# Means of v by TensorE, summary rows in one product a head, a later index step and another tile for the hidden row, in an attention and two-MoE kernel

## The chip, the core and the metric

The kernel runs on one core of a Trainium2 chip. A core has engines that run side by side, each through its own list of instructions in a fixed order: TensorE (PE, with its weight loads as PEld), VectorE (DVE), ScalarE (ACT), GpSimd (POOL) and SyncE (SP), whose queue here issues most of the loads. They meet by semaphores. The metric is the device time of one execution in microseconds, as the median of several runs.

## The reference

Three layers over 2 x 768 tokens with 512 columns (8 heads of 64). First an attention of two parts: each query sees the keys within 15 places of it, and one summary for each of 24 blocks of 32 tokens. A block's key summary is the maximum, its value summary the mean:

```python
k_sum = k.reshape(B, H, nb, block, D).max(axis=3)
v_sum = v.reshape(B, H, nb, block, D).mean(axis=3)
scores_s = scale * np.einsum('bhsd,bhnd->bhsn', q, k_sum) + np.log(block)
scores_all = np.concatenate([scores_l_m, scores_s], axis=-1)   # softmax over both
return np.matmul(a, np.concatenate([v, v_sum], axis=2))
```

Then a dense layer, `max(x @ w1, x @ w2, x @ w3) @ w_out`, and a mixture of 8 experts: a token with a positive skip score goes through `relu(xc @ w1[e]) @ w2[e]` of its best expert, times the gate's weight, plus itself; other tokens stay as they are.

## The kernel before

**Work units.** The 1536 tokens are four groups u of 384 (groups 0 and 1 are the first sequence, b = 0). In attention the heads go in four pairs p, two heads on 128 partitions. Per group and pair: keys and queries are loaded, `scores` makes products of 64 queries with 96 keys and 24 summaries, softmax follows (`ttr` on VectorE, `ex` on ScalarE, `rec` on VectorE, `norm` on POOL), `turn` transposes the weights on TensorE, `turned` copies them to SBUF (ps), and `pv` multiplies them with the values. For `pv` a block's values are a window tile vx of 120 rows: 96 rows of v, loaded (L227), and below them 24 rows of summaries, which ScalarE copies in once for each of six blocks (`fill_v`, L250). Those summaries come from the whole v of the pair, transposed (`load_v`, 384 KB), summed by VectorE (`sum_v`, L205), turned by TensorE (`sum_t`, L210) and scaled by ScalarE (`sum_o`). They serve both groups of a sequence.

**The dense layer** runs over the result in high and low float32r parts: 18 chains of 12 products a group (`chain`, L367), each after its weights are split on ScalarE, POOL and VectorE (`w_c1` to `w_c5`, L334 to L360) from 512 KB chunks. In the first group's first chain each part (`cp`) follows one head pair. To keep TensorE busy while there is little for it, 63 products of a zero tile are made at the start (`warm_up`, L185), in 20 groups.

**What sets the order.** Up to the experts, each piece of work is an entry (`op`) with an engine, a duration, a key, what it comes after, and the buffers it takes and frees. `arrange` simulates the engines with those durations, always takes the ready piece with the smallest key, and the order that comes out is the order in which every engine gets its instructions. On the DMA queue a piece without a free buffer holds up all behind it. The warm-up groups are such pieces too, with keys 0 to 19; `att` gives the pieces of attention.

**Experts.** Written out by hand: the most frequent expert's tokens go in pairs of 128-token tiles (`pair`) and a last `single`, another expert's in a `single`, and up to 32 tokens left over from a third expert (the remainder) in `tail`, spread over the steps of a pair: `tail_x` (L995 to L997) makes an index on VectorE and fetches rows by POOL. With FAST2 the pair has a second remainder. In `single` the hidden row, 128 x 512 for each half, is written by ScalarE to `hr`, turned by TensorE and split.

Of the kernel before, what the change touches and what calls it, by code (L numbers as in the profile page):

```python
# [8 lines left out]
F32 = mybir.dt.float32  # L9
# [9 lines left out]
B, H, S, D = 2, 8, 768, 64  # L19
P = 128  # L20
NPR = H // 2
QB = 64
NBK = S // QB
KW = 96
NS = 24
KT = KW + NS
G = 384
BPG = G // QB
TPG = G // P
# [116 lines left out]
def build(tc, a, out):  # L146
    nc = tc.nc
# [3 lines left out]
    psM = ctx.enter_context(tc.tile_pool(name="psM", bufs=3, space=PSUM))  # L151
# [4 lines left out]
    ax_ = actx.enter_context(tc.tile_pool(name="ksvs", bufs=1, side="right"))  # L156
# [44 lines left out]
    def sum_v(b, p):  # L201
# [3 lines left out]
        nc.vector.tensor_reduce(vs[:, KW:], vt, AX.X, ALU.add)  # L205
        ST["vs", b, p] = vs

    def sum_t(b, p):
        ST["pvs", b, p] = psM.tile([P, 512], F32, name="pm")
        nc.tensor.transpose(ST["pvs", b, p][:KT, :P], ST["vs", b, p], ident)  # L210
# [89 lines left out]
    def pv(u, p):  # L300
        vx = ST["vx", u, p]
        po = psO.tile([P, G], F32, name="po")
        for i in range(BPG):
            for h in range(2):
                nc.tensor.matmul(po[64 * h:64 * h + 64, i * QB:(i + 1) * QB], vx[:, i, 64 * h:64 * h + 64],
                                 ST["ps", u, p, h][:, i * QB:(i + 1) * QB], start=True, stop=True)
        ST["po", u, p] = po
# [258 lines left out]
    ONE = {}  # L566
# [205 lines left out]
    def op(name, eng, dur, key, fn, *args, after=(), take=(), uses=(), lag=0.0):  # L772
        OPS.append(dict(name=name, eng=eng, dur=dur, key=key, fn=fn, args=args, after=after, take=take, uses=uses, lag=lag))

    def att(u, p, s, t, o):
        b, half = divmod(u, 2)
        e = (u, p)
        pre = s - 12 if u else -100.0 + 10 * p
        if half == 0:
            ek = EARLY_KV.get((b, p))  # L780
            op(("lk", b, p), "DMA", 1.35, pre, load_k, b, p, take=[(ek[0] if ek else "raw", ("kt", b, p))])
            op(("sk", b, p), "DVE", 0.87, s - 3, sum_k, b, p, after=[("lk", b, p)], take=[(f"ks{p}", ("ks", b, p))],
               uses=[("kt", b, p)])
        if u == 0:
            op(("lkx",) + e, "DVE", 1.0, s - 2.5, windows, p, after=[("lk", b, p)],
               take=[(EARLY_X[e][0] if e in EARLY_X else "kx", ("kx",) + e)], uses=[("kt", 0, p)])
        else:
            op(("lkx",) + e, "DMA", 1.25, pre + 0.1, load_x, u, p, "k", take=[(EARLY_X[e][0] if e in EARLY_X else "kx", ("kx",) + e)])
        op(("lq",) + e, "DMA", 0.68, pre + 0.2, load_x, u, p, "q", take=[("qt", ("qt",) + e)])
        if half == 0:  # L790
            op(("lv", b, p), "DMA", 1.35, pre + 0.3, load_v, b, p, take=[(ek[1] if ek else "raw", ("vt", b, p))])
            op(("sv", b, p), "DVE", 0.92, s - 2, sum_v, b, p, after=[("lv", b, p)],
               take=[("vs", ("vs", b, p))], uses=[("vt", b, p)])
            op(("st", b, p), "PE", 0.2, s + 1, sum_t, b, p, after=[("sv", b, p)], take=[("pm", ("pvs", b, p))],
               uses=[("vs", b, p)])
            op(("so", b, p), "ACT", 0.17, s + 1, sum_o, b, p, after=[("st", b, p)], take=[(f"v1{p}", ("v1", b, p))],
               uses=[("pvs", b, p)])
        op(("lvx",) + e, "DMA", 1.0, pre + 0.4, load_x, u, p, "v", take=[(EARLY_X[e][1] if e in EARLY_X else "vx", ("vx",) + e)])
        op(("fk",) + e, "DVE", 0.15, s - 1, fill_k, u, p, after=[("lkx",) + e, ("sk", b, p)], uses=[("ks", b, p)])
        op(("fv",) + e, "ACT", 0.8, t, fill_v, u, p, after=[("lvx",) + e, ("so", b, p)],  # L800
           uses=[("v1", b, p)])
        for h in range(2):
            g = e + (h,)
            if h == 0:
                op(("sc",) + e, "PE", 0.8, s, scores, u, p, after=[("fk",) + e, ("lq",) + e],
                   take=[(f"{z}{i}", (z,) + e + (i,)) for z in ("sc", "pr") for i in range(2)], uses=[("kx",) + e, ("qt",) + e])
            op(("tt",) + g, "DVE", 0.61, s + 0.5 + 0.1 * h, ttr, u, p, h, after=[("sc",) + e, ("mask",)], uses=[("sc",) + g])
            op(("ex",) + g, "ACT", 1.14, s + 0.6 + 0.1 * h, ex, u, p, h, after=[("tt",) + g])
            op(("rc",) + g, "DVE", 0.36, s + 0.7 + 0.1 * h, rec, u, p, h, after=[("ex",) + g])
            op(("nm",) + g, "Pool", 0.82, s + 0.8 + 0.1 * h, norm, u, p, h, after=[("rc",) + g])  # L810
            op(("tu",) + g, "PE", 0.33, t + 0.1 * h, turn, u, p, h, after=[("nm",) + g], take=[(f"pt{h}", ("pt",) + g)],
               uses=[("pr",) + g])
            op(("td",) + g, "ACT", 0.43, t + 0.2 + 0.1 * h, turned, u, p, h, after=[("tu",) + g],
               take=[(f"ps{h}", ("ps",) + g)], uses=[("pt",) + g])
        op(("pv",) + e, "PE", 0.86, o, pv, u, p, after=[("td",) + e + (0,), ("td",) + e + (1,), ("fv",) + e],
           take=[("po", ("po",) + e)], uses=[("ps",) + e + (0,), ("ps",) + e + (1,), ("vx",) + e])
        tk = [("xh", ("xh", u)), ("xl", ("xl", u))] if p == 0 else []
        op(("ph",) + e, "ACT", 0.38, o + 0.3, put_h, u, p, after=[("pv",) + e], take=tk)
        op(("pl",) + e, "DVE", 0.51, o + 0.4, put_l, u, p, after=[("ph",) + e], uses=[("po",) + e])

    op(("mask",), "DMA", 0.5, -99.75, load_mask)
    op(("consts",), "DMA", 0.45, 30, load_consts)
    op(("tri",), "DVE", 0.15, 36, put_tri, after=[("consts",)])
    op(("table",), "Pool", 0.5, 50.0, clear_table, take=[("cx", ("table",))], lag=2.0)
# [146 lines left out]

    xn, inx, xth, xtl, ph, ptx = (M2[z] for z in ("xn", "inx", "xth", "xtl", "ph", "ptx"))
    xr, yo, xm = ([mp.tile([P, DM], F32, name=f"{z}{i}") for i in range(2)] for z in ("xr", "yo", "xm"))
    hr = [xr[1], xm[1]]
    ic, isc, im = (mp.tile([P, 2, 2], I32, name=z) for z in ("ic", "isc", "im"))
    hth, htl = ([mp.tile([P, 512], F32R, name=f"{z}{i}") for i in range(2)] for z in ("hth", "htl"))
    py = [psM.tile([P, 512], F32, name="pm") for _ in range(2)]
# [84 lines left out]

    def pair(p, t, spl=0, gen=None):
        begin(2)
        if spl:
            tail_x(spl)
        tails = TAILS2 if spl == FAST2 else TAILS
        hv = [(hth[b // 2][:, b % 2 * 2 * P:(b % 2 + 1) * 2 * P], htl[b // 2][:, b % 2 * 2 * P:(b % 2 + 1) * 2 * P])
              for b in range(4)]

        def first(f):
            ps = ph[f % 3][:, :2 * P]
            n, o = 0, f % 4 * P
            for i, r in ((0, xth), (1, xth), (0, xtl)):
                for d in range(KC1):
                    w = M2["w", p, 2 * d + f // 4][i]
                    nc.tensor.matmul(ps, w[:, o:o + P], r[:, d, :], start=(n == 0), stop=(n == 3 * KC1 - 1))  # L1077
                    n += 1
            hh, hl = hv[f % 4]
            nc.scalar.activation(hh, ps, AF.Relu)  # L1080
            nc.vector.scalar_tensor_tensor(hl, ps, 0.0, hh.bitcast(F32), ALU.max, ALU.subtract)  # L1081

        def second(f):
            hh, hl = hv[f % 4]
            wh, wl = M2["w", p, 8 + f]
            for i in range(2):
                o = i * P
                for n, (l, r) in enumerate(((hh, wh), (hh, wl), (hl, wh))):
                    nc.tensor.matmul(py[i], l[:, o:o + P], r, start=(f == 0 and n == 0), stop=(f == 7 and n == 2))  # L1089
        first(0)  # L1090
        if gen:
            nc.gpsimd.tensor_copy(inx, M2["in2"])
            fetch()
        first(1)
        for f in range(8):
            if f == 5:
                turn_x()
            if f + 2 < 8:
                first(f + 2)
            if f == 5:  # L1100
                next_x(t + 2)
            second(f)
            if gen and f < 4:
                for _ in range(2):
                    next(gen, None)
                if f == 3:
                    ids("in2", row(1))
            if spl:
                for c in PSPL[f] if spl != FAST2 else ():
                    split(c, 1 - p)  # L1110
                if f in tails:
                    tail(tails[f])
        end(2)

    def single(p, t, spl=0, last=False):
        begin(1)
        if spl:
            tail_x(spl)
# [112 lines left out]
    def most():  # L1231
# [13 lines left out]
            with tc.If(VK[0] > 8):  # L1245
                pair(0, b0 + 4)
        with tc.If((VK[0] & 1) == 0):
            single(0, l0)
        with tc.If(VK[1] > 1):  # L1249
            single(1, b1 + 1, last=True)  # L1250

    def any_ranks():
        for k in range(NE):
# [13 lines left out]
def host_inputs(inputs):  # L1267
# [2 lines left out]
    t = lambda z: np.ascontiguousarray(z.transpose(0, 1, 3, 2)).reshape(B, NPR, P, S)  # L1270
    r["qt"] = t(q)
    r["vt"] = t(v)
    r["kt"] = t(k)
    kt = np.zeros((B, NPR, P, S + 32), np.float32)
    kt[..., 16:16 + S] = r["kt"]
# [52 lines left out]
```

## Time and profile before

| what | value |
| --- | --- |
| median of 3 runs | 462.48 us (461.01 to 465.97) |
| profiled execution | 463.62 us |
| its span, first to last instruction | 461.7 us |
| mean granted TensorE clock | 0.989 |
| TensorE busy | 429.7 us, 93% |
| VectorE, ScalarE, POOL busy | 244.0, 197.7, 133.0 us |
| DMA moved | 58.31 MB, 126 GB/s on the mean |

In the page a group of instructions has line, engine, operation, what it writes and reads, shape and count; times are in us from the span's start. A row of the timeline gives start, length, engine, line and operation, and in brackets how long the engine was idle before it and what ended the wait. The length of a product contains its way through the array, so products that follow each other closely overlap; the distance of their starts is what one costs. A float32 product is recorded as two passes, a turn as one.

### The profile page before, as it was taken

How to read it: one execution, taken by the hardware profiler on the slowest of the kernel's cores; microseconds unless marked ns; L12 is line 12 of the kernel's file. 1: busy time of each engine (PE TensorE's matmuls, PEld its weight loads, DVE VectorE, ACT ScalarE, POOL GpSimd, SP SyncE). 2: the span in 40 equal slices, each digit the busy share in tenths (PEclk: the TensorE clock that was granted, in tenths of full speed). 3: DMA queues.
4: the chain of work that ended last, by engine and by line, in shares of the span. 5: the costliest groups of instructions: out<-in, count | busy, mean ns of one | idle time of the engine just before them, and what ended most of it. 6: DMA issues, size and time to landing. Idle time of an engine off the chain costs nothing. (4 is left out here: it accounts for less than half of the span.)

```text
span 461.7 us, 9459 instructions
## 1 busy us (share of the span) xinstructions
PE 429.7 (93%) x3423; PEld 385.6 (84%) x3427; DVE 244.0 (53%) x760; ACT 197.7 (43%) x523; POOL 133.0 (29%) x185
## 2 busy tenths in 40 slices
PE   6977779999998999999999999999999989999892
PEld 2556669999998989999999998998999879797781
DVE  4988999989943353345114174585137621413220
ACT  2799986755464482357211173211116411111220
POOL 2233453323112440433102412142224123232230
PEclk9999989999999999999999999999999999999996
DMA  8993624576525264121021190314911480010100
GB/s 240 261 307 133 244 102 156 175 244 232 177 84 190 93 197 118 27 98 27 3 99 39 44 351 19 137 11 160 333 50 49 154 280 26 22 48 25 49 18 29
DMA packets 28245, 58.31 MB, mean 126 GB/s; under 512 B 6527, under 2 KB 8831, under 8 KB 28184
## 3 DMA queue, kind: packets, MB, share of 16 engines
q1 hardware_dynamic: 25384, 51.19, 34.3%
q0 software_dynamic: 2800, 6.37, 4.3%
q8 instruction: 31, 0.51, 0.5%
q14 instruction: 30, 0.25, 0.2%
HBM read 48.43 MB, written 10.47 MB: 128 GB/s over the span
## 5 line engine op out<-in xcount | busy, mean ns | idle before, releaser
L367 PE MATMUL pm<-xh,wh 128*128 128x384 f32 x288 | 65.7, 348 | 2.5 <-DVE t L376 1.4
L367 PE MATMUL pm<-xh,wl 128*128 128x384 f32 x288 | 63.1, 339 | 0.0
L367 PE MATMUL pm<-xl,wh 128*128 128x384 f32 x288 | 62.9, 339 | 0.0
L1080 ACT ACTIVATE hth<-ph 128x256 fp32r<-128x256 f32 x40 | 15.4, 384 | 90.5 <-PE ph L1077 86.2
L367 PEld LDWEIGHTS pm<-xh,wh 128*128 128x128 f32 x288 | 49.3, 188 | 4.7 <-DVE t L376 1.9
L367 PEld LDWEIGHTS pm<-xh,wl 128*128 128x128 f32 x288 | 51.7, 190 | 0.3 <-DVE wl L360 0.3
L367 PEld LDWEIGHTS pm<-xl,wh 128*128 128x128 f32 x288 | 51.6, 189 | 0.0
L1081 DVE SCALAR_TENSOR_TENSOR htl<-ph,hth 128x256 fp32r<-128x256 f32 x40 | 16.6, 422 | 57.6 <-ACT hth L1080 57.6
L376 DVE TENSOR_TENSOR t<-pm,t 128x384 f32<-128x384 f32 x48 | 26.4, 552 | 37.9 <-PE pm L367 37.1
L287 POOL TENSOR_TENSOR pr<-pr,se 128x360 f32<-128x360 f32 x32 | 26.1, 822 | 69.7 <-DVE se L283 52.6
L394 PE MATMUL pm<-wh,h 128*128 128x262 f32 (+1 forms) x288 | 42.8, 288 | 1.3 <-ACT v L214 1.1
L277 ACT ACTIVATE pr<-pr,mx 128x120 f32<-128x120 f32 x96 | 36.6, 384 | 10.3 <-DVE mx L271 10.2
L384 POOL TENSOR_TENSOR h<-t,h 128x384 fp32r<-128x384 f32 x24 | 26.2, 1098 | 49.1 <-ACT h L381 47.6
L394 PEld LDWEIGHTS pm<-wh,h 128*128 128x128 f32 x288 | 37.9, 189 | 2.2 <-ACT v L214 1.3
L1089 PE MATMUL pm<-wh,htl 128*128 128x512 f32 x80 | 31.6, 395 | 1.3 <-DVE htl L1081 1.3
L711 POOL DMA_INDIRECT xn<-x2d,inx x16 | 17.0, 1060 | 53.8 <-DVE xm L1043 24.2
L1089 PE MATMUL pm<-wh,hth 128*128 128x512 f32 x80 | 31.8, 398 | 0.0
L1089 PE MATMUL pm<-wl,hth 128*128 128x512 f32 x80 | 31.4, 393 | 0.0
L342 POOL TENSOR_SCALAR cx<-cx 128x512 f32<-128x512 f32 x24 | 18.5, 771 | 36.3 <-ACT cx L334 32.2
L555 POOL DMA_INDIRECT table<-rtab,rsi x12 | 11.9, 996 | 58.8 <-DVE rsi L550 36.9
L381 ACT CAST h<-t 128x384 fp32r<-128x384 f32 x24 | 11.9, 513 | 35.5 <-DVE t L376 34.1
L1077 PE MATMUL ph<-xth,wh 128*128 128x256 f32 x160 | 26.3, 286 | 0.0
(307 smaller groups left out, 852.5 us busy)
## 6 DMA issues: line engine op xcount, KB each, us to landing
raw<-in_m SPq DMA_DIRECT2D x48, 256.0 KB, 4.7
raw<-in_wx SPq DMA_DIRECT2D x22, 512.0 KB, 4.2
kx<-in_kx SPq DMA_DIRECT2D x12, 360.0 KB, 3.9
vx<-in_vx SPq DMA_DIRECT2D x14, 288.0 KB, 4.0
qt<-in_qt SPq DMA_DIRECT2D x16, 192.0 KB, 5.1
x2d<-raw SPq DMA_DIRECT2D x12, 256.0 KB, 3.3
raw<-in_kt SPq DMA_DIRECT2D x7, 384.0 KB, 9.4
raw<-in_vt SPq DMA_DIRECT2D x7, 384.0 KB, 5.0
```

The source lines that it names most:

```text
L277: nc.scalar.activation(pr[:, t, :], pr[:, t, :], AF.Exp, bias=mx[:, t:t + 1], scale=-1.0, accum_out=se[:, t:t + 1])
L287: nc.gpsimd.tensor_tensor(pr, pr, se.unsqueeze(2).broadcast_to([P, TPG, KT]), ALU.mult)
L342: nc.gpsimd.tensor_scalar(x, x, HIGH, LOW, ALU.min, ALU.max)
L367: nc.tensor.matmul(ST["ch", u, f, j], l[j, f][:, c * P:(c + 1) * P], r[u][:, c, :], start=(cs[0] == 0 and n == 0), stop=(cs[-1] == KC1 - 1 ...
L376: nc.vector.tensor_tensor(ST["t1", u, f], ps, ST["t1", u, f], ALU.max)
L384: nc.gpsimd.tensor_tensor(HL[u, f], ST["t1", u, f], HH[u, f].bitcast(F32), ALU.subtract)
L394: nc.tensor.matmul(ps, l[u, f][:, t * P:(t + 1) * P], r[3, f][:, lo:hi], start=(part != 1 and n == 0), stop=(part != 0 and n == len(ops) - 1))
L711: nc.gpsimd.indirect_dma_start(out=xn[t], out_offset=None, in_=x2d, in_offset=bass.IndirectOffsetOnAxis(ap=inx[:, t, 0:1], axis=0), bounds ...
L1077: nc.tensor.matmul(ps, w[:, o:o + P], r[:, d, :], start=(n == 0), stop=(n == 3 * KC1 - 1))
L1080: nc.scalar.activation(hh, ps, AF.Relu)
L1081: nc.vector.scalar_tensor_tensor(hl, ps, 0.0, hh.bitcast(F32), ALU.max, ALU.subtract)
L1089: nc.tensor.matmul(py[i], l[:, o:o + P], r, start=(f == 0 and n == 0), stop=(f == 7 and n == 2))
```

## The change

Three edits.

1. For the first sequence the means of v are made by TensorE from what is loaded: 6 products with the window tiles of group 0 (first half) and 3 with the second half of v, loaded by rows (`vn`, 192 KB for a pair in place of 384), against slices of a constant `band` with 1/32 in it. ScalarE copies the 24 rows out. In `pv` of group 0 the summaries are no more rows of the window tiles: one product of 24 rows by 384 columns a head opens the sum, and the 12 products of 96 rows add to it. `fill_v` is left out for group 0; group 1 and the second sequence keep theirs. Keys stay as they were, but for those of the two pieces that make the means.
2. In the pair with FAST2, `tail_x` follows the second step of the second layer in place of standing ahead of the pair.
3. The two singles of `most` get raw tiles as `hr` in place of `xr[1], xm[1]`.

```diff
+    def load_band():
+        ONE["band"] = ax_.tile([P, 46 + 32], F32, name="band")
+        nc.sync.dma_start(ONE["band"], a["band"])
+    def load_w(b, p):
+        ST["v", b, p] = hp.tile([P, S // 2], F32, name="h1") if (b, p) in EARLY_KV else raw_tile([P, S // 2])
+        nc.sync.dma_start(ST["v", b, p], a["vn"][p])
+    def mean_v(b, p):
+        ST["pvs", b, p] = psM.tile([P, 512], F32, name="pm")
+        band = ONE["band"]
+        w = [(band[:KW, 22 - 2 * i:22 - 2 * i + NS], ST["vx", 2 * b, p][:KW, i, :]) for i in range(BPG)]
+        w += [(band[:, 46 + 8 - 4 * c:46 + 8 - 4 * c + NS], ST["v", b, p][:, c * P:(c + 1) * P]) for c in range(TPG)]
+        for n, (l, r) in enumerate(w):
+            nc.tensor.matmul(ST["pvs", b, p][KW:KT, :P], l, r, start=(n == 0), stop=(n == len(w) - 1))
+    def mean_o(b, p):
+        VS[b, p] = ax_.tile([KT, P], F32, name=f"v1{p}")
+        nc.scalar.copy(VS[b, p][KW:KT], ST["pvs", b, p][KW:KT, :P])
...
         po = psO.tile([P, G], F32, name="po")
+        if u == 0:
+            for h in range(2):
+                nc.tensor.matmul(po[64 * h:64 * h + 64, :], VS[0, p][KW:KT, 64 * h:64 * h + 64], ST["ps", u, p, h][KW:KT, :],
+                                 start=True, stop=False)
+            for i in range(BPG):
+                for h in range(2):
+                    nc.tensor.matmul(po[64 * h:64 * h + 64, i * QB:(i + 1) * QB], vx[:KW, i, 64 * h:64 * h + 64],
+                                     ST["ps", u, p, h][:KW, i * QB:(i + 1) * QB], start=False, stop=(i == BPG - 1))
...
+            if b == 0:
+                op(("lv", b, p), "DMA", 0.68, pre + 0.3, load_w, b, p, take=[(ek[1] if ek else "raw", ("vt", b, p))])
...
+                op(("st", b, p), "PE", 1.9, s - 1, mean_v, b, p, after=[("lv", b, p), ("band",), ("lvx",) + e], take=[("pm", ("pvs", b, p))],
+                   uses=[("vt", b, p)])
+                op(("so", b, p), "ACT", 0.17, s - 0.9, mean_o, b, p, after=[("st", b, p)], take=[(f"v1{p}", ("v1", b, p))],
+                   uses=[("pvs", b, p)])
...
-        op(("fv",) + e, "ACT", 0.8, t, fill_v, u, p, after=[("lvx",) + e, ("so", b, p)],
-           uses=[("v1", b, p)])
+        if u:
+            op(("fv",) + e, "ACT", 0.8, t, fill_v, u, p, after=[("lvx",) + e, ("so", b, p)],
+               uses=[("v1", b, p)])
...
-        op(("pv",) + e, "PE", 0.86, o, pv, u, p, after=[("td",) + e + (0,), ("td",) + e + (1,), ("fv",) + e],
+        op(("pv",) + e, "PE", 0.86 if u else 1.9, o, pv, u, p, after=[("td",) + e + (0,), ("td",) + e + (1,), ("fv",) + e if u else ("so", b, p)],
...
+    op(("band",), "DMA", 0.3, -98.5, load_band)
...
-    hr = [xr[1], xm[1]]
+    HR = [xr[1], xm[1]]
...
-        if spl:
+        if spl and spl != FAST2:
             tail_x(spl)
...
             second(f)
+            if spl == FAST2 and f == 1:
+                tail_x(spl)
...
-            single(0, l0)
+            single(0, l0, hr=M2["raw"])
         with tc.If(VK[1] > 1):
-            single(1, b1 + 1, last=True)
+            single(1, b1 + 1, last=True, hr=M2["raw"])
```

The order that the planner gives TensorE, around the last pv of group 0 and the first of group 1. Before (sc, pt and po are scores, turned weights and pv; pm with xh is a part of a chain; t is the warm-up's zero tile):

```order
L305 MATMUL po<-ps_611,h_386 64x64
L367 MATMUL pm<-xh,wh_0_582 128x384
L367 MATMUL pm<-xl,wh_0_582 128x384
L367 MATMUL pm<-xh,wl_0_590 128x384
L292 MATMUL pt_683<-ident,pr_535 120x128 x3
L292 MATMUL pt_690<-ident,pr_538 120x128 x3
```

The change at the same place, from the products of the summary rows (L327) on:

```order
L327 MATMUL po<-ps_609,v_447 64x384
L327 MATMUL po<-ps_634,v_447 64x384
L331 MATMUL po<-ps_609,h_341 64x64
...
L185 LDWEIGHTS t_101
L185 MATMUL pm<-t_101 128x512
...
L399 MATMUL pm<-xh,wh_0_562 128x384
L399 MATMUL pm<-xl,wh_0_562 128x384
L399 MATMUL pm<-xh,wl_0_595 128x384
L185 LDWEIGHTS t_101
L185 MATMUL pm<-t_101 128x512
...
L337 MATMUL po<-ps_707,vx 64x64
```

Between the parts of the first chain now stand warm-up groups of three products, and group 1's first pv (L337) comes after two parts of the chain, where it came after three; the warm-ups were all ahead of the chain before.

VectorE in the pair with FAST2, before (yo is the output of the pair ahead, mo the remainder's index, htl a low half):

```order
L1052 SCALAR_TENSOR_TENSOR yo_4009<-pm,ic,xr_4007 128x512
L995 TENSOR_SCALAR mo<-mi,con 128x1
L996 COPY mo<-mi 128x1
L1081 SCALAR_TENSOR_TENSOR htl_4017<-ph_3497,hth_4015 128x256
L1081 SCALAR_TENSOR_TENSOR htl_4017<-ph_3498,hth_4015 128x256
```

The change:

```order
L1095 SCALAR_TENSOR_TENSOR yo_4035<-pm,ic,xr_4033 128x512
L1124 SCALAR_TENSOR_TENSOR htl_4043<-ph_3523,hth_4041 128x256
L1124 SCALAR_TENSOR_TENSOR htl_4043<-ph_3524,hth_4041 128x256
L1124 SCALAR_TENSOR_TENSOR htl_4044<-ph_3525,hth_4042 128x256
L1124 SCALAR_TENSOR_TENSOR htl_4044<-ph_3523,hth_4042 128x256
L1038 TENSOR_SCALAR mo<-mi,con 128x1
L1039 COPY mo<-mi 128x1
```

The index step has moved from ahead of the first low half to behind the fourth.

ScalarE in the first single, with what each row waits for, before:

```order
L1247 COMPARE_AND_BRANCH
L1132 ACTIVATE xr_4007<-ph_3497 128x512 [waits DVE_49,PE_49,Pool_49]
L1137 CAST hth_4015<-ph_3499 128x512 [waits PE_49,Activation_49]
L1132 ACTIVATE xm_4011<-ph_3498 128x512 [waits PE_49]
L1137 CAST hth_4016<-ph_3497 128x512 [waits PE_49,Activation_49]
```

The change:

```order
L1292 COMPARE_AND_BRANCH
L1177 ACTIVATE raw_3504<-ph_3523 128x512 [waits DMAHW2_49,DVE_49,PE_49]
L1182 CAST hth_4041<-ph_3525 128x512 [waits PE_49,Activation_49]
L1177 ACTIVATE raw_3505<-ph_3524 128x512 [waits DMAHW3_49,DVE_49,PE_49]
L1182 CAST hth_4042<-ph_3523 128x512 [waits PE_49,Activation_49]
```

The hidden row's first half has a wait for a load in place of the one for POOL.

## Rows read from the trace of the kernel before

**Rows 1.** Table of stretches: busy us of each engine, clock, DMA.

```profile
core 0: us, PE busy (x) PEld busy (x) DVE busy (x) ACT busy (x) POOL busy (x), PEclk, DMA share, GB/s
9.50:42.27 32.77, 27.35 (x330) 17.62 (x335) 28.71 (x131) 29.48 (x94) 10.61 (x17) 1.00 0.81 235
42.27:64.78 22.51, 17.32 (x175) 14.90 (x175) 21.28 (x62) 21.29 (x64) 10.08 (x13) 1.00 0.58 199
64.78:69.42 4.64, 4.64 (x40) 4.13 (x38) 4.61 (x8) 2.86 (x6) 2.89 (x3) 0.63 0.33 113
69.42:130.00 60.58, 59.78 (x388) 59.38 (x384) 55.71 (x92) 35.72 (x68) 16.70 (x20) 1.00 0.56 188
```

**Rows 2.** Timeline, second pair: start, length, engine, line [idle before, what ended it].

```profile
377.47 0.21 DVE L995 TENSOR_SCALAR mo<-mi,con 128x1 int32<-128x1 int32 x1 [3.89 <-DMA out<-yq,mo]
...
378.13 0.51 PE L1089 MATMUL pm<-wh,htl 128*128 128x512 f32 x1 [1.31 <-DVE htl L1081]
```

**Rows 3.** Timeline of the second pair: the remainder's gather and its first use.

```profile
385.09 1.07 POOL L997 DMA_INDIRECT mask<-x2d,mo  x1 [0.16 <-issue]
...
390.54 0.27 PE L1005 MATMUL pm<-ident,mask 128*128 128x128 f32 x1
```

**Rows 4.** DMA issues: KB, us to landing (gather of 385.09, load of 2.59).

```profile
mask<-x2d,mo POOLq DMA_INDIRECT x1, 2.5
...
vx<-in_vx SPq DMA_DIRECT2D x1, 288.0 KB, 7.0
```

**Rows 5.** Timeline of the first single: ScalarE and TensorE.

```profile
431.14 0.60 ACT L1132 ACTIVATE xr<-ph 128x512 f32<-128x512 f32 x1 [8.77 <-POOLq L1245]
431.80 0.66 PE L1136 MATMUL ph<-ident,xr 128*128 128x128 f32 x4 [1.23 <-ACT xr L1132]
```

**Rows 6.** Timeline of the prelude.

```profile
8.41 0.95 DVE L205 TENSOR_REDUCE vs<-raw 128x24 f32<-128x768 f32 x1 [2.70 <-DMA raw<-in_vt]
...
9.65 3.40 PE L185 MATMUL pm<-t 128*128 128x512 bf16 x14
...
12.88 0.49 PE L292 MATMUL pt<-ident,pr 128*120 128x128 f32 x3
...
13.21 0.81 PE L185 MATMUL pm<-t 128*128 128x512 bf16 x3
...
14.56 0.85 PE L258 MATMUL sc<-kx,qt 64*64 64x120 f32 x24
15.34 0.32 PE L210 MATMUL pm<-ident,vs 128*120 128x128 f32 x1
15.59 0.92 PE L305 MATMUL po<-ps,vx 120*64 120x64 f32 x24
...
16.44 2.76 PE L185 MATMUL pm<-t 128*128 128x512 bf16 x11
...
39.91 0.42 PE L367 MATMUL pm<-xh,wh 128*128 128x384 f32 x1
...
40.60 1.12 PE L305 MATMUL po<-ps,vx 120*64 120x64 f32 x24
```

**Rows 7.** Groups to 70 us: count, busy, mean ns, idle before.

```profile
L250 ACT COPY vx<-v 24x768 f32<-24x768 f32 x6 | 5.0, 830 | 0.2
```

**Rows 8.** Timeline, second pair: full-width turns, products on 32-column tiles.

```profile
390.65 1.04 PE L698 MATMUL ptx<-ident,xn 128*128 128x128 f32 x8
391.44 0.71 PE L1077 MATMUL ph<-xth,wh 128*128 128x256 f32 x4
...
399.49 1.96 PE L1021 MATMUL pm<-raw,hqt 128*32 128x128 f32 x64
401.37 0.74 PE L1077 MATMUL ph<-xth,wh 128*128 128x256 f32 x4
```

**Rows 9.** Waits of SP's queue to 60 us: total, times, longest us.

```profile
SPq L227 <- PE po L305: 17.4, 2, 10.6
```

More of the change, by code (lines that the diff above doesn't have):

```diff
@@ L302, in pv @@
         po = psO.tile([P, G], F32, name="po")
+        if u == 0:
[6 more added lines that the diff above has]
+                                     ST["ps", u, p, h][:KW, i * QB:(i + 1) * QB], start=False, stop=(i == BPG - 1))
+            ST["po", u, p] = po
+            return
         for i in range(BPG):
@@ L789, in att @@
         op(("lq",) + e, "DMA", 0.68, pre + 0.2, load_x, u, p, "q", take=[("qt", ("qt",) + e)])
+        op(("lvx",) + e, "DMA", 1.0, pre + 0.4, load_x, u, p, "v", take=[(EARLY_X[e][1] if e in EARLY_X else "vx", ("vx",) + e)])
         if half == 0:
-            op(("lv", b, p), "DMA", 1.35, pre + 0.3, load_v, b, p, take=[(ek[1] if ek else "raw", ("vt", b, p))])
-            op(("sv", b, p), "DVE", 0.92, s - 2, sum_v, b, p, after=[("lv", b, p)],
-               take=[("vs", ("vs", b, p))], uses=[("vt", b, p)])
@@ L794, in att @@
[L794 to L798, printed above, removed]
+            if b == 0:
+                op(("lv", b, p), "DMA", 0.68, pre + 0.3, load_w, b, p, take=[(ek[1] if ek else "raw", ("vt", b, p))])
+            else:
+                op(("lv", b, p), "DMA", 1.35, pre + 0.3, load_v, b, p, take=[(ek[1] if ek else "raw", ("vt", b, p))])
@@ new lines, in att @@
+            if b == 0:
+                op(("st", b, p), "PE", 1.9, s - 1, mean_v, b, p, after=[("lv", b, p), ("band",), ("lvx",) + e], take=[("pm", ("pvs", b, p))],
+                   uses=[("vt", b, p)])
+                op(("so", b, p), "ACT", 0.17, s - 0.9, mean_o, b, p, after=[("st", b, p)], take=[(f"v1{p}", ("v1", b, p))],
+                   uses=[("pvs", b, p)])
+            else:
+                op(("sv", b, p), "DVE", 0.92, s - 2, sum_v, b, p, after=[("lv", b, p)],
+                   take=[("vs", ("vs", b, p))], uses=[("vt", b, p)])
+                op(("st", b, p), "PE", 0.2, s + 1, sum_t, b, p, after=[("sv", b, p)], take=[("pm", ("pvs", b, p))],
+                   uses=[("vs", b, p)])
+                op(("so", b, p), "ACT", 0.17, s + 1, sum_o, b, p, after=[("st", b, p)], take=[(f"v1{p}", ("v1", b, p))],
+                   uses=[("pvs", b, p)])
@@ L814, in att @@
                take=[(f"ps{h}", ("ps",) + g)], uses=[("pt",) + g])
-        op(("pv",) + e, "PE", 0.86, o, pv, u, p, after=[("td",) + e + (0,), ("td",) + e + (1,), ("fv",) + e],
-           take=[("po", ("po",) + e)], uses=[("ps",) + e + (0,), ("ps",) + e + (1,), ("vx",) + e])
+        op(("pv",) + e, "PE", 0.86 if u else 1.9, o, pv, u, p, after=[("td",) + e + (0,), ("td",) + e + (1,), ("fv",) + e if u else ("so", b, p)],
+           take=[("po", ("po",) + e)], uses=[("ps",) + e + (0,), ("ps",) + e + (1,), ("vx",) + e] + ([] if u else [("v1", b, p)]))
         tk = [("xh", ("xh", u)), ("xl", ("xl", u))] if p == 0 else []
@@ L1113, in pair, with single @@
         end(2)
-    def single(p, t, spl=0, last=False):
+    def single(p, t, spl=0, last=False, hr=HR):
         begin(1)
@@ L1272, in host_inputs @@
     r["vt"] = t(v)
+    r["vn"] = v[0].reshape(NPR, 2, S // P, P, D).transpose(0, 3, 2, 1, 4).reshape(NPR, P, S)[..., S // 2:]
+    r["band"] = np.zeros((P, 46 + 32), np.float32)
+    w = np.arange(16, 80)
+    r["band"][w, 22 + (w - 16) // 32] = 1.0 / 32.0
+    r["band"][np.arange(P), 46 + 20 + np.arange(P) // 32] = 1.0 / 32.0
     r["kt"] = t(k)
```

## The prediction, made before the changed kernel had run

> **What bounds the kernel now.** I read the table of stretches first, then the order of time at the places that the edit touches, then the waits of the SP queue. The table shows two kernels in one [rows 1]. From 69.42 us on TensorE is the bound, busy 59.78 of 60.58 us to 130 and hardly less until the last tiles: whatever makes TensorE later before 69 us makes the end later by as much. Before 42.27 us, in the prelude (attention of the first group, ahead of the first full weight chain), no engine is full and three are close: VectorE 28.71 and ScalarE 29.48 of 32.77 us, TensorE 27.35, throw-away warm-up products among it. Between 42.27 and 64.78 us VectorE and ScalarE are both 95% busy and TensorE is idle for 5.2 of 22.51 us: the preparation of the weights sets the pace there. From 64.78 to 69.42 the granted clock of TensorE is 0.63 on average, in part the lower of its two levels, 1.2 GHz, after that idling; at 2.4 GHz 4.64 x 0.37 = 1.7 us would be saved.
>
> **The tail: two waits.** In the second pair of tiles VectorE comes to the remainder's index step (L995) while the last remainder scatter is still under way, stands until 377.47, the low halves (L1081) queue behind it, and TensorE loses 1.31 us [rows 2]. The change puts the step behind the fourth low half, whose columns come only after that gap, near 380 us, when the scatter has landed: **-1.31**. The gather that uses the index is issued by POOL at 385.09, behind POOL's own scatters, so it doesn't move; it lands 2.5 us later, 387.6, and TensorE wants it at 390.54 - 1.31 = 389.2 [rows 3, 4]. That is 1.6 us of cover; without it the gap opens again at L1005. In the first single tile ScalarE may write its hidden row (L1132) only once POOL has passed the branch at L1245, 431.14, and TensorE loses 1.23 us [rows 5]. In the change the row goes to a raw tile; it then waits for VectorE, TensorE and a load that is long done, no more for POOL: **-1.23**. What is late next there is the low half behind ScalarE (L1138), which TensorE doesn't meet until it has other columns done. Tail **-2.5**.
>
> **The prelude: what goes.** Four reductions of v on VectorE at 0.95 us, 3.8 us [rows 6]; four broadcasts on ScalarE at 0.83, 3.3 us [rows 7]; four turns of the sums on TensorE, 0.25 each from start to start, 15.34 to 15.59 [rows 6]; loads of 4 x 192 KB less the band's 40 KB, 0.75 MB, which at the stretch's 235 GB/s are 3.2 us [rows 1]. It all lies beside other work and pays only where those engines are waited for, not TensorE. POOL loses four short clears that nobody waits for.
>
> **What comes.** A mean of v is nine float32 products of 128 columns, two passes each, in one tile of 32 columns. The trace has no such row; the nearest is the remainder's L1021, of that width and type: 64 passes of 128 columns, four abreast, from 399.49 to 401.37, so 16 in a row in 1.88 us, 0.1175 each; 18 make **2.1** [rows 8]. Lower end: three turns of 128 columns, one pass each, take 0.33 (12.88 to 13.21), nine 1.0. Upper end: 18 lone ones at 0.49 / 3 = 0.163, 2.9 [rows 6]. I take 2.1 for the type and width.
>
> The same row prices the change of tile: eight full-width passes of 128 columns take 0.79 (390.65 to 391.44), 0.099 each [rows 8], 16 would take 1.58, and L1021 takes 0.3 more than that. The Trainium skill (TensorEngine Tiling (Array Packing), Key Properties) says that changing the tiling mode drains TensorE, which speaks against this change, as it enters such a mode eight more times. The row agrees, with 0.3 us; without it a mean would be 1.8.
>
> The weighted sum (pv) of a head pair was 24 passes, 15.59 to 16.44, 0.85 us [rows 6]. It keeps them, on 96 rows in place of 120, and gets two products of 384 columns. One pass of those is 3 x 0.1175 = 0.35; the two heads write different columns, so the four passes overlap by one and take 1.05: **+1.05**, 1.9 in all (+0.7 if side by side throughout, +1.4 if not at all). Per head pair 2.1 - 0.25 + 1.05 = 2.9; four make 11.6 us more on TensorE.
>
> **Where it lies.** The prelude has 32.77 - 27.35 = 5.4 us of idle TensorE [rows 1]; 11.6 can't hide in it. Nor do the warm-ups step aside, for they stand in a fixed order, and the planner now puts ten groups of three behind the first group's last turn, ahead of the first chain, where there were none. I add up the change's order from the first mean to the second group's first pv: 4 means 8.4, 4 pv 7.6, 5 scores at 0.78 3.9, 10 turns at 0.33 3.3, 14 warm-up groups at 3 x 0.231 9.7, 2 partial chains at 0.69 1.4 [rows 6]: 34.3 us. It begins when the first vx has landed, 2.59 + 7.0 = 9.6, less 0.8 for the halved load ahead of it, and the band after it, 0.2: 9.0 [rows 4, 1]. That pv starts at 43.3 in place of 40.60: **+2.7**. Then come itself, three warm-up groups, two turns and two partial chains, 5.0 us, so the first full chain starts at 48.3 in place of 42.27: **+6.0**.
>
> The stretch to 70 us can give some back: 5.2 us of idling and 1.7 of low clock. It can't give back the weights. The vx load of the second group's third head pair waits up to 10.6 us for just that pv to free its buffer [rows 9], and the fifth weight chunk stands behind it on SP. So weights from there on come 2.7 us later, and VectorE and ScalarE have no room at 95%. I take +3.5, near the lower end, since there the weights are waited for and not TensorE. After 69 us it stays.
>
> **Sum.** +3.5 - 2.5 = +1.0. The profiled execution took 463.62 us (span 461.7), so 464.6 by it; it stands 1.1 above the median of the three runs, 462.48, so **463.5** by the median.
>
> **Rivals.** (1) The relief wins. If a product is one pass, a mean takes 1.0 and pv 0.55 less; the sum falls by 4 x 1.65 = 6.6 and that pv could start at 36.7. Then VectorE, ScalarE and the loads decide, with 3.2 to 3.8 us less to do, and the first softmax step, which stood behind the reduction's wait of 2.70 us for v [rows 6], comes that much sooner. It decides once a mean costs under 1.4, where that pv comes no later than before. Against it: only turns take one pass here. Prelude between 0 and -3: 460.0 to 457.0, middle 459.
> (2) Nothing is given back, the other side of a gain: TensorE is full from 9 to 57 us, the clock falls all the same, and 6.0 stays: 466.0, and with means of 2.9 us 3.2 more, 469.2. For it: the idling after 42 us hangs on weights that are later too. It decides when the chains, not the weights, are last at 70 us.
> (3) The tail's waits come back elsewhere (the index step behind another scatter, the raw tile behind a load), so the change doesn't do that part: 462.48 + 3.5 = 466.0. Against it: the landings above.
>
> **Chances.** Forecast 0.46 (its own range 461.3 to 465.6), rival 1 0.22, rival 2 0.22, rival 3 0.07, something else 0.03. The range 459.5 to 467.5 leaves out the far ends of rivals 1 and 2, about a tenth each. Under 1%, 4.6 us, a measurement of this kernel can't tell from no change. Faster by more (under 457.9) is the far end of rival 1, 0.06; slower by more (over 467.1) the far end of rival 2, 0.12; within, 0.82.
>
> **What would show it.** Right: nine L223 products in 1.9 to 2.3 us; TensorE without gaps from 9 to 48 us; the second group's first pv near 43, the third vx load just behind it; the first full chain near 48; no wait for POOL at L1177, and low halves of the second pair without a wait ahead of the third. Wrong: short means and a first chain before 44 (rival 1), or TensorE's work 6 us late at 70 us (rival 2).

## The result and the profile after

The change took **466.56 us** in the median of 20 runs (463.64 to 470.63), the kernel before 462.59 us (20 runs, 459.56 to 465.97): ratio 1.0086, 95% interval 1.0066 to 1.0106, so 4.0 us slower (3.1 to 4.9). The forecast was 463.5 with a range of 459.5 to 467.5: the time lies inside, 3.1 above the middle. The profiled execution of the change took 469.08 us (span 467.3), 2.5 above its median; that of before 1.0 above its own. Between the two spans lie 5.6 us.

The table of stretches, with the bounds and columns of [rows 1]:

```profile
9.50:42.27 32.77, 32.33 (x371) 20.80 (x375) 25.85 (x121) 25.36 (x87) 11.05 (x14) 1.00 0.67 205
42.27:64.78 22.51, 20.48 (x208) 17.25 (x207) 16.84 (x55) 17.55 (x51) 8.13 (x9) 1.00 0.59 198
64.78:69.42 4.64, 3.26 (x23) 2.81 (x20) 4.54 (x11) 4.45 (x13) 3.11 (x4) 1.00 0.41 119
69.42:130.00 60.58, 58.09 (x350) 55.84 (x349) 54.81 (x90) 34.91 (x66) 18.22 (x22) 0.97 0.58 188
```

In the prelude TensorE has gone from 27.35 to 32.33 of 32.77 us; its 5.4 us of idle time are used up, and VectorE and ScalarE have 2.9 and 4.1 us less to do there. From 42.27 to 64.78 us, where those two were 95% busy, they now wait, and TensorE, busy 20.48 us of it, is the engine that is nearly full.

TensorE's timeline at the places that answer to [rows 6]: the first mean, the first weighted sum, the second group's first weighted sum, the first full chain.

```profile
8.39 1.47 PE L223 MATMUL pm<-vx,band 96*24 96x128 f32 x12 [1.38 <-DMA band<-in_band]
9.70 0.82 PE L223 MATMUL pm<-raw,band 128*24 128x128 f32 x6
10.45 0.39 PE L185 MATMUL pm<-t 128*128 128x512 bf16 x1
...
19.01 0.86 PE L327 MATMUL po<-ps,v 24*64 24x384 f32 x4
19.80 0.92 PE L331 MATMUL po<-ps,vx 96*64 96x64 f32 x24
20.65 0.32 PE L313 MATMUL pt<-ident,pr 128*120 128x128 f32 x1
...
42.21 0.92 PE L337 MATMUL po<-ps,vx 120*64 120x64 f32 x24
...
46.74 0.85 PE L399 MATMUL pm<-xh,wh 128*128 128x384 f32 x4
```

A mean takes 10.45 - 8.39 = 2.06 us, the summary rows' products 19.80 - 19.01 = 0.79, the whole weighted sum 1.64. The second group's first weighted sum is 1.6 us later than before, the first full chain 4.5.

The tail's two places ([rows 2] and [rows 5]), timeline of VectorE, ScalarE and TensorE:

```profile
384.61 0.39 PE L1132 MATMUL pm<-wh,htl 128*128 128x512 f32 x1
384.77 0.42 DVE L1124 SCALAR_TENSOR_TENSOR htl<-ph,hth 128x256 fp32r<-128x256 f32 x1 [1.01 <-ACT hth L1123]
387.58 0.42 DVE L1124 SCALAR_TENSOR_TENSOR htl<-ph,hth 128x256 fp32r<-128x256 f32 x1 [2.39 <-ACT hth L1123]
387.92 0.20 DVE L1038 TENSOR_SCALAR mo<-mi,con 128x1 int32<-128x1 int32 x1
...
436.22 0.60 ACT L1177 ACTIVATE raw<-ph 128x512 f32<-128x512 f32 x1 [6.82 <-PE ph L1175]
437.42 0.60 PE L1181 MATMUL ph<-ident,raw 128*128 128x128 f32 x4
```

The index step (L1038) starts without a wait, right behind the fourth low half; ScalarE's hidden row now waits for TensorE's own columns and no longer for POOL; TensorE goes on without a gap at both places. That is what the change was to do there. Yet the tail as a whole isn't shorter, and the reason is a third place, the start of the third pair of tiles (TensorE's timeline, then the table of stretches, then the DMA queues from 349 to 350.2 us):

```profile
347.64 0.39 PE L1132 MATMUL pm<-wh,htl 128*128 128x512 f32 x1
350.14 0.93 PE L1120 MATMUL ph<-xth,wh 128*128 128x256 f32 x4 [2.12 <-issue]
```

```profile
348.00:352.00 4.00, 1.89 (x11) 1.89 (x11) 1.09 (x4) 0.00 (x0) 1.54 (x3) 0.81 0.58 189
352.00:356.00 4.00, 4.00 (x28) 4.00 (x28) 0.85 (x2) 0.77 (x2) 1.00 (x1) 0.77 0.11 39
```

```profile
q8 instruction: 1, 0.02, 9.7%
```

TensorE stops for 2.12 us and waits for nothing that the profile shows ("issue"). Here it leaves the first branch's body (the two pairs under `EA > EARLY`) and jumps over the `Else`; the test for `others`, another branch, stands just behind, and no row tells the two apart. (Pairs are counted here from the first, at 300.9 us; the second pair of [rows 2], with FAST2, is the fourth.) A packet of instructions moves at just that time. Behind the stop part of the work runs at the lower level, 1.2 GHz: 4 x 0.19 + 4 x 0.23 = 1.7 us lost. The waits of TensorE from 340 us on, of the kernel before, show no such stop, and the two waits that the change takes away:

```profile
PE pm L1089 <- DVE htl L1081: 1.3, 1, 1.3
PE ph L1136 <- ACT xr L1132: 1.2, 1, 1.2
PE ph L1130 <- DVEq L1245: 1.0, 1, 1.0
```

One place cuts every profile in two: the first product of the first pair of tiles (L1077 before, L1120 in the change). Its row, of before, the change, and the change in a second execution (first and last start in us; the rest of the span is what lies behind it):

```profile
L1077 PE MATMUL ph<-xth,wh x160: 277/281/387, 296.7 to 419.7; 128*128 128x256 f32 x160
```

```profile
L1120 PE MATMUL ph<-xth,wh x160: 277/281/419, 300.9 to 426.8; 128*128 128x256 f32 x160
```

```profile
L1120 PE MATMUL ph<-xth,wh x160: 277/282/553, 300.5 to 426.6; 128*128 128x256 f32 x160
```

So of the 5.6 us between the spans 4.2 arise before that place and 1.4 behind it: 467.3 - 300.9 = 166.4 against 461.7 - 296.7 = 165.0. These 1.4 are 2.1 for the stop, 1.7 for the clock and some -2.5 for the two waits.

### The profile page after: what moved, and what is told of

Its sections match the earlier page's. It is cut to its first block, busy times and chain, and to the rows that moved or that the text cites. A ratio compares the mean times of both kernels' runs of the same rounds, so it can differ in the third digit from the quotient of the medians.

```text
span 467.3 us, 9619 instructions
## 1 busy us (share of the span) xinstructions
PE 442.2 (95%) x3506; PEld 394.5 (84%) x3511; DVE 238.2 (51%) x756; ACT 194.3 (42%) x519; POOL 132.8 (28%) x181
## 5 line engine op out<-in xcount | busy, mean ns | idle before, releaser
L1120 PE MATMUL ph<-xth,wh 128*128 128x256 f32 x160 | 27.0, 291 | 2.1 <-issue 2.1
L1120 PEld LDWEIGHTS ph<-xth,wh 128*128 128x128 f32 x160 | 23.7, 193 | 4.7 <-issue 2.9
```

## The experiments

Each ratio is against the kernel before on the same chip. "Head" is the first product of the first pair of tiles, "rest" the span behind it, "stream" the instructions that TensorE's stream has more than before ahead of the branch (a float32 product is four: two loads and two passes, as L223's 18 records for nine products show; a turn is two, one load and one pass; so the means are 144, the four turns that go -8, the summary products 32). The profiles, which lack some records, hold 166 instructions more for the change and 139 for the means alone. The expectations below count a turn as four, so their 128, 160, 256, 262 and 100 are each 8 too low; the argument doesn't hang on that.

| kernel | head us | rest us | stop us | stream | ratio (95%) |
|---|---|---|---|---|---|
| before | 296.7 | 165.0 | none | 0 | 1 |
| the change | 300.9 | 166.4 | 2.1 | 168 | 1.0086 (1.0066 to 1.0106) |
| the change, second profile | 300.5 | 166.4 | 2.5 | 168 | |
| tail edits alone | 297.1 | 162.6 | none | 0 | 0.9967 (0.9935 to 0.9999) |
| without the tail edits | 304.0 | 164.8 | 2.5 | 168 | 1.0122 (1.0073 to 1.0171) |
| means alone, with the tail | 300.0 | 164.3 | 2.2 | 136 | 1.0029 (0.9996 to 1.0061) |
| weighted sum alone, with the tail | 297.2 | 163.1 | none | 32 | 0.9987 (0.9958 to 1.0016) |
| the change, stream moved | 300.7 | 162.5 | none | 264 | 1.0014 (0.9987 to 1.0040) |
| before, stream moved | 296.8 | 164.9 | 2.1 | 150 | 1.0011 (0.9984 to 1.0039) |
| the change, ten warm-ups | 294.3 | 163.5 | 1.7 | 108 | 0.9940 (0.9913 to 0.9968) |
| the same, stream moved | 291.5 | 163.2 | none | 270 | **0.9905** (0.9872 to 0.9939) |
| tail edits and ten warm-ups | 301.6 | 162.4 | none | -60 | 1.0032 (1.0001 to 1.0062) |

**1. The tail edits alone**, on the kernel before:

```diff
         begin(2)
-        if spl:
+        if spl and spl != FAST2:
             tail_x(spl)
...
             second(f)
+            if spl == FAST2 and f == 1:
+                tail_x(spl)
...
-            single(0, l0)
+            single(0, l0, hr=M2["raw"])
...
```

> The kernel before with the two edits of the tail alone (index step behind the fourth low half, hidden rows of the single tiles in raw tiles); the prelude is the old one. Theory A (the two waits were worth what they showed, and the prelude costs +3.5 to +4.2): 462.6 - 1.3 - 1.2 = 460.1. Theory B (the waits come back elsewhere in the tail, so that all of the +4.0 is the prelude's): 462.6. Theory C (the tail gives 2.5 and the prelude costs 6.5 in the median, more than the +4.2 that the profiled execution shows at 300 us): 460.1 as A; the next kernel tells A from C.

Measured 461.85 us against 463.06, ratio 0.9967. Both waits are gone and the rest is 2.4 us shorter (162.6 for 165.0). The median gain of some 1.5 us is less than 2.5, with an interval from 0 to 3.0, which by itself hardly tells A from B; in this profile a gather that landed late cost 0.9. Theory B falls by the profile: the waits do not come back as such.

**2. Without the tail edits** (the two edits above undone in the change):

> The change without its two tail edits. Theory A: 462.6 + 3.5 to 4.2 = 466.1 to 466.8. Theory B: 466.6, the same as the whole change. Theory C: 462.6 + 6.5 = 469.1. In the profile, TensorE's work at 296 to 300 us stood 4.2 us later than before; the 2.1 us stop of TensorE at 348 us, which waits for nothing that the profile shows, and the 1.2 GHz stretch behind it are gone if they were chance, and there again if they hang on the place in the instruction stream, which is the same here up to the second pair of tiles.

469.19 us, 1.0122; the interval of these six runs holds all three theories. The stop is there again, 2.5 us, so it wasn't chance. What nobody expected is in the waits of TensorE from 350 us on:

```profile
PE ph L1120 <- issue: 2.5, 1, 2.5
PE ph L1173 <- DVEq L1288: 1.0, 1, 1.0
PE pm L1064 <- DVE hqt L1059: 0.2, 1, 0.2
```

The two old waits, 1.3 and 1.2 us, are not there, although their code is. They were waits for a scatter of POOL's and for POOL's branch [rows 2, 5]; with TensorE 2.5 us later both are over in time. The stop takes their place: the rest is 164.8 us, as long as before. This run's head is 7.3 us late; 1.8 of that is a clock of 0.93 from 20 to 30 us and 0.91 from 30 to 42 (10 x 0.07 + 12 x 0.09).

**3. The means alone**: the old broadcast and the old weighted sum, the rest as in the change.

```diff
-        if u == 0:
+        if False:
...
-        if u:
+        if True:
             op(("fv",) + e, "ACT", 0.8, t, fill_v, u, p, after=[("lvx",) + e, ("so", b, p)],
...
-        op(("pv",) + e, "PE", 0.86 if u else 1.9, o, pv, u, p, ...
+        op(("pv",) + e, "PE", 0.86, o, pv, u, p, ...
```

> The change with the old weighted sum: the means of v come from TensorE products, but ScalarE copies them into the blocks again and the weighted sum has its 24 passes and no products of its own for the summary rows. Of the change's added TensorE work of 4 x (2.06 - 0.25 + 0.79) = 10.4 us, 7.2 stay. Theory A (idle TensorE takes up some 6 us, the rest stays): prelude +1.0, with the tail's -2.5 461.1. Theory C (each part of the work costs in proportion, 6.5 x 7.2 / 10.4 = 4.5): 464.6.

464.64 us, 1.0029 (+1.3 us). Both theories were wrong in their working: the head is 3.3 us late, more than A's 1.0, and the stop (2.2 us) was in neither. That C's 464.6 came out is luck.

**4. The weighted sum alone**: VectorE reduces v as before, the summary rows stay in one product a head.

```diff
-            if b == 0:
+            if False:
                 op(("lv", b, p), "DMA", 0.68, pre + 0.3, load_w, ...
...
-    op(("band",), "DMA", 0.3, -98.5, load_band)
```

> The change with the old sums of v: VectorE reduces the whole v and TensorE turns the sums, as before, but the weighted sum takes the summary rows in one product a head. Of the added TensorE work of 10.4 us, 4 x 0.79 = 3.2 stay. Theory A: idle TensorE takes it up, prelude 0, with the tail's -2.5 460.1. Theory C: 6.5 x 3.2 / 10.4 = 2.0, so 462.1. If ScalarE's four broadcasts (3.3 us), which this leaves out, were waited for: below 460.1.

462.15 us, 0.9987. The head is 0.5 us late and there is no stop; C's time, 462.1, comes out without the 2.0 us in the prelude that it rests on. By the heads, 3.3 against 0.5 us, it is the means that cost. But the profile of the means alone shows a clock of 0.83 from 10 to 20 us, where the kernel before has 1.00 (10 x 0.17 = 1.7 us), and by the ratios, against the 0.9967 of the tail edits, the means cost 2.9 us with the stop's 2.2 among them, and the weighted sum 0.9. So the stop comes with the means; how the rest divides between the halves is not shown.

**5. The change with its stream moved** by 96 instructions, with the same columns of warm-up:

```diff
-    def warm_up(n):
+    def warm_up(n, k=1):
         pw = psM.tile([P, 512], F32, name="pm")
-        for _ in range(n):
-            nc.tensor.matmul(pw, warm[:, :P], warm, start=True, stop=True)
+        c = 512 // k
+        for _ in range(k * n):
+            nc.tensor.matmul(pw[:, :c], warm[:, :P], warm[:, :c], start=True, stop=True)
...
-        op(("wu", i), "PE", 0.216 * n, 1.0 * i, warm_up, n, ...
+        op(("wu", i), "PE", 0.216 * n, 1.0 * i, warm_up, n, 2 if i < 15 else 1, ...
```

> The whole change; in the first 15 warm-up groups each product of 512 columns stands as two of 256: the same columns, 96 more instructions (48 loads and 48 products) in TensorE's stream. So far TensorE stopped for 2.1 to 2.5 us at the start of the third pair of tiles, where it comes out of a branch that skips code, in the kernels whose stream is 128 (the means alone) or 160 instructions longer ahead of that branch, and not in those where it is 0 or 32 longer. Theory P (the stop hangs on the place of the branch in TensorE's instruction stream): with 256 more than before it goes: 466.6 - 2.2 = 464.4, down to 462.9 if the 1.2 GHz stretch behind it goes too; no wait of TensorE at that place. Theory Q (the stop comes from the means' work itself or from the later time): 466.6 and the stop is there. The Trainium skill (Runtime: NRT & Kernel Launch, Instruction fetch mechanics) says that instructions come in blocks of 256 and that a taken branch whose target is not among the blocks held must wait for a DMA, which is theory P.

1.0014 in place of 1.0086: 3.3 us come back. All that TensorE waits for from 340 us on is

```profile
PE ph L1176 <- DVEq L1291: 1.0, 1, 1.0
```

and the rest is 162.5 us. Theory P: the stop hangs on the branch's place in TensorE's instruction stream.

**6. The kernel before with its stream moved**, by 150 instructions (the same `warm_up`, with `4 if i in (1, 2) else 2`):

> The kernel before; its warm-up products stand as two of 256 columns, in two of the groups as four of 128: the same columns, 150 more instructions in TensorE's stream, nothing else. Theory P: the stop of 2.1 to 2.5 us appears at the third pair of tiles: 462.6 + 2.2 = 464.8, up to 466.5 with a stretch of 1.2 GHz behind it. Theory Q: 462.6 and no stop.

The stop is there, in a kernel that has nothing of the change (waits of TensorE from 340 to 350 us, and from 350 on):

```profile
PE ph L1078 <- SPq L1325: 2.1, 1, 2.1
```

```profile
PE ph L1131 <- DVEq L1246: 1.0, 1, 1.0
PE pm L1090 <- DVE htl L1082: 0.6, 1, 0.6
```

So theory P holds on the other side too. But the time hardly moves, 1.0011, where P said +2.2: of the old waits' 2.5 us only 0.6 are left, 1.9 of the stop's 2.1 are taken up, and the rest is 164.9 us. (The profile puts an SP line here as releaser; the same stop is "issue" in the change.)

**7. The change with ten warm-up groups** in place of twenty (`range(10)`, last group 9):

> The whole change with 10 warm-up groups in place of 20; the order, made by the same rules, then has none of the ten that stood ahead of the first full chain. Theory W (what is late at 300 us, 4.2 us, is TensorE's own work ahead of the first chains): 10 x 3 x 0.231 = 6.9 us less of it, the first full chain near 42 in place of 46.7, the work at 300 us 3.0 to 4.2 sooner: 463.6 to 462.4. Theory V (the weights are late, through the vx load that waits for the second group's first weighted sum, and through VectorE and ScalarE): a gain of 1.4 at most, the lateness of that load: 465.2. Its stream is 60 instructions shorter than the change's, 100 longer than before; under theory P the stop at the third pair may be there or not, and 2.2 more go if it isn't. If the clock falls for want of work in the prelude: above 466.6.

461.44 us against 464.2, 0.9940: faster than both kernels. The head is 6.6 us sooner than in the change, though 30 products of 0.231 us, 6.9 us, are all that went. Theory V falls by the SP queue's timeline, the vx load that waits for the weighted sum and the weight chunk behind it, of before, of the change and of this one:

```profile
41.79 0.33 SPq L227 DMA_DIRECT2D vx<-in_vx  x1
...
42.64 0.42 SPq L327 DMA_DIRECT2D raw<-in_wx  x1
```

```profile
43.20 0.33 SPq L248 DMA_DIRECT2D vx<-in_vx  x1
...
44.05 0.42 SPq L359 DMA_DIRECT2D raw<-in_wx  x1
```

```profile
41.45 0.33 SPq L248 DMA_DIRECT2D vx<-in_vx  x1
...
43.61 0.42 SPq L359 DMA_DIRECT2D raw<-in_wx  x1
```

The weight chunk comes only 0.4 us sooner than in the change, and the work 6.6; it comes 1.0 later than before, and the work 2.4 sooner. The 6.6 are also more than theory W's 3.0 to 4.2; why is open. The stop is there, 1.7 us, and here the profile names VectorE:

```profile
PE ph L1120 <- DVE yo L1095: 1.7, 1, 1.7
PE ph L1175 <- DVEq L1290: 1.0, 1, 1.0
```

VectorE's piece (L1095, from 340.78 us on for 1.44) was over 0.9 us before TensorE went on at 343.13, so it was not what TensorE stood for to the end.

**8. The same with the stream moved** by 162 more (`4 if i < 8 else 1`):

> The change with 10 warm-up groups in place of 20, and in the first eight of them each product of 512 columns as four of 128: 162 more instructions, so that TensorE's stream is 262 longer than before ahead of the branch, in place of 100. With 100 the stop at the third pair of tiles was there, 1.7 us, and the time 0.994 of before. Theory P: the stop is gone, and with the two waits of the tail taken away nothing absorbs what that gives: 0.994 x 464.2 - 1.7 = 459.7, a ratio of 0.990. Rival: something behind it takes it up (a gather that lands late, as in the kernel with the tail edits alone): 0.994. If the narrow products fill TensorE less in the prelude and the clock falls: above 0.994.

459.38 us against 464.36, **0.9905**, the best version: 4.4 us faster than before (2.8 to 5.9). No stop; its head row:

```profile
L1121 PE MATMUL ph<-xth,wh x160: 277/281/387, 291.5 to 413.9; 128*128 128x256 f32 x160
```

Theory P's time came out, 0.990, but in this profile not in its way: the head is 2.8 us sooner than in the seventh run (294.3), and the rest only 0.3 us shorter, 163.2 for 163.5, though a stop of 1.7 is gone. TensorE's waits from the head on are these, where the seventh run had the stop and 1.0 us for the branch:

```profile
PE ph L1176 <- DVEq L1291: 1.5, 1, 1.5
PE pm L1059 <- ACT hq L1056: 0.4, 1, 0.4
PE ptx L731 <- DMA xn<-x2d,inx: 0.3, 1, 0.3
```

They take up 1.2 of the 1.7 us, much as the rival said. That the stop goes with the place is shown here once more; that its going made this kernel the faster one is not.

**9. The kernel before with the tail edits and ten warm-up groups**, to see what the means and products are worth then:

> The kernel before with the two tail edits and 10 warm-up groups in place of 20: no means on TensorE, the old weighted sum. It tells what the first part of the change is worth once the warm-up groups no longer stand ahead of the first chain. Theory M (the products earn what they free on VectorE and ScalarE): this one is slower than the change with 10 groups by 1 to 3 us; the tail's 2.5 off the time before gives a ratio of 0.9945, and its prelude hardly gains, since TensorE had 5.4 us of idle time there: 0.993 to 0.9945. Theory N (TensorE's free time is all that counts): fewer warm-ups give it as much here as there, 0.988 to 0.990, at or under the change with 10 groups. If the clock falls in the prelude, where TensorE then has less to do: 0.995 and above. Its stream is 60 instructions shorter than before; whether the stop comes there no run shows yet.

465.89 us, 1.0032: not M's 0.993 nor N's 0.988, but the third case. The prelude's stretches, of this kernel and then of the eighth (columns as in [rows 1]):

```profile
20.00:30.00 10.00, 6.46 (x61) 4.79 (x62) 6.58 (x32) 8.22 (x25) 3.71 (x6) 0.50 0.95 278
30.00:42.00 12.00, 8.86 (x114) 6.93 (x112) 10.61 (x44) 11.12 (x37) 4.04 (x6) 0.78 0.62 194
42.00:50.00 8.00, 8.00 (x76) 6.80 (x73) 7.04 (x26) 7.20 (x23) 3.12 (x3) 0.68 0.17 50
```

```profile
20.00:30.00 10.00, 10.00 (x156) 7.41 (x152) 7.52 (x40) 9.29 (x35) 5.20 (x7) 1.00 0.85 266
30.00:42.00 12.00, 11.66 (x161) 8.32 (x160) 11.57 (x49) 11.90 (x36) 3.49 (x5) 1.00 0.46 146
42.00:50.00 8.00, 7.46 (x64) 6.72 (x62) 6.31 (x25) 7.83 (x27) 2.93 (x4) 1.00 0.78 257
```

Without the change's first part TensorE has too little to do once the warm-ups go: it idles, its clock stands at 1.2 GHz all the way from 20 to 30 us, and the head is 4.9 us late. With it TensorE is full of its own work and stays at 2.4 GHz there.

**10. The change once more**, one execution:

> The change once more, for a second profile. Theory P: the stop of TensorE at the third pair of tiles is there again, 2 to 2.5 us. The work at the head of the first pair of tiles (before 296.7 us; the change 300.9) should stand at 300 to 302 us if the clock holds at 2.4 GHz; the first profile's 1.8 us of low clock right behind the stop should be there again if the stop brings it, and not if that was chance.

The stop is there, 2.5 us; the head is at 300.5; and the low clock behind the stop came again: 0.72 from 348 to 352 us and 0.85 from 352 to 356, 1.7 us lost. In the other four kernels with a stop the clock behind it was 1.00.

## Why the prediction was right where it was, and where it failed

- **Tail, -2.5: right.** Wherever there is no stop the rest is 162.4 to 163.2 us with the tail edits and 165.0 without, -1.8 to -2.6; the times of run 1 give -1.5, with an interval from 0 to -3.0. The gather at L1048 had its cover.
- **A mean at 2.1: right**, 2.06. **The weighted sum at +1.05: too much**, 0.79; the two heads' products ran almost side by side, the +0.7 that the text kept as lower end. Together 10.4 us more on TensorE, not 11.6.
- **Where it lies: right.** TensorE is full from 8.4 to 62 us. The second group's first weighted sum came at 42.2 for 43.3, the first full chain at 46.7 for 48.3; four sums at 0.26 less and a start 0.6 sooner are 1.6 us, the second difference and more than the first.
- **+3.5 stays: near in size, wrong in its reason.** At the head 4.2 and 3.8 us in the two profiles; by the ratios of two kernels that have the tail edits and no stop, 1.0014 with the prelude's edit and 0.9967 without, 2.2 us, give or take 1.9. The text took them for the weights' lateness, through the third vx load (1.4 us late, not 2.7). The seventh run shows that TensorE's own queue was late, warm-ups among it: 6.9 us of them less, 6.6 us sooner, with weights 0.4 sooner.
- **The sum, +1.0: failed, for want of a term.** The median is +4.0. The step that failed is "What comes", and with it the sum: 168 instructions were counted in time alone and not in place. They moved the branch behind the second pair so that the jump stops TensorE for 2.1 to 2.5 us. Moved on to 264, the same work is 1.0014, +0.6 us (-0.6 to +1.9), and the forecast's +1.0 lies in that: the missing term, stop and slow stretch together, is 3.3 of the 4.0 us.
- **And the tail hid how it came about.** In the kernel before the same stop costs next to nothing, since two waits, for a scatter of POOL's and for POOL's branch, take it up. The change takes those waits away and brings the stop at once. By the ratios the tail gives 1.5 us, the stop with its slow stretch takes 3.3 and the prelude 2.2, which make the 4.0; in the one profile of the change the same terms are -2.5, 2.1 + 1.7 and 4.2, and this execution was 2.5 us above the median.
- **Rivals.** Rival 2's time, 466.0, is near the result by luck: 3.8 to 4.2 us were late at the head, not 6.0 (7.3 in the run without the tail edits, with a low clock in the prelude), and the stop makes up the rest. But the condition it named, that TensorE's own work and not the weights is last, is what the seventh run found. Rival 1 fell with a mean at 2.06 us. Rival 3 fell as it was put; that something else in the tail would take the gain was near what came.

The Trainium skill (Runtime: NRT & Kernel Launch, Instruction fetch mechanics) says that instructions are fetched in blocks of 256 and that a taken branch to a target outside the blocks held waits for a DMA. The runs agree in that the stop comes and goes with the place: none at -60, 0 and 32 instructions, a stop at 108, 136, 150 and 168, none at 264 and 270. They fit a period of 256, but only one stretch of stops was seen. In three pairs of kernels the same work was timed at two places, and the stop came or went each time. That the stop *is* a wait for that DMA is inferred, not shown, and the packets do not decide it. A packet of instructions starts within the stop in five of the six profiles that have one; in the seventh run's, from 341.4 to 343.2 us, none moves. And in the fifth run, which has no stop, one moves just ahead of the third pair, from 346 to 348.3 us, while TensorE works on:

```profile
q8 instruction: 1, 0.02, 2.5%
```

Open: why the clock fell behind the stop in the change alone, and why the head of the ten-group version with its stream moved is 5.2 us sooner than before while the weighted sum alone, whose first full chain starts sooner (38.1 us against 40.8), gains nothing at the head. The spread of the heads of one prelude (300.5, 300.9, 304.0) says that differences of some 3 us between single profiles carry little.

## What to carry to other kernels

Where a kernel jumps over code, adding or taking away instructions ahead of the jump can cost or save a stop at a place that the edit doesn't touch; look at waits just behind branches ("issue" in three of the six profiles here, an unrelated line in the others), and time the edit with its stream moved as well before judging it. A wait that is taken away may have been the cushion for another delay, so two edits of equal size can cancel or not by what stands between. Work added to keep an engine's clock up can become a cost once real work fills that engine: try to take it out when you put the work in, and look at the clock, for without the real work the same step made this kernel's head 4.9 us later.

## What the hardware showed that was not expected

- Behind one jump over code TensorE stops for 1.7 to 2.5 us or not at all, with the same code on both sides, by its place in the stream (six profiles of five kernels with, six without). What that is worth depends on what follows: the rest of the span was 3.9 us longer in the change (166.4 against 162.5, a slow clock of 1.7 us among it) and no longer in the kernel before (164.9 against 165.0).
- 96 more loads and products in narrower pieces, for the same columns, cost the prelude nothing that shows: head 300.7 against 300.5 and 300.9.
